# Scores and attend on 64-row array tiles for four heads at a time, with the attention written as seven rounds per group

## Chip, cores and metric

The kernel runs on one core of a Trainium2 chip. The metric is device time in microseconds of one execution of the program. Engine names below: PE is TensorE (PEld its weight loads), DVE is VectorE, ACT is ScalarE, POOL is GpSimd, SP is SyncE, which here only issues DMAs.

## What is computed

Two stages, one after the other. First attention over 8 batches of 12 heads, 448 tokens, 64 elements per head: q and k are normalised by their root mean square and scaled by `g_q` and `g_k`, then softmax of the scores times v. Its output, 3584 tokens of 768, goes through a layer of experts: a dense two-layer network for all tokens, plus one of 8 experts per token, chosen by the largest of 8 logits and weighted by its softmax probability.

```python
q_n, k_n = rmsnorm(q, g_q), rmsnorm(k, g_k)
attn = softmax(scale * q_n @ k_n.T)            # per batch and head
x = (attn @ v) as (3584, 768)
y = relu(x @ w1_dense) @ w2_dense              # 768 -> 512 -> 768
e = argmax(x @ w_gate, axis=1)
y[n] += gate[n] * (relu(x[n] @ w1[e[n]]) @ w2[e[n]])
```

## The kernel before, in words

**Tiling of the attention.** The unit is a pair of heads, `t`, 48 in all, 6 in a batch; loads go by groups of two pairs (four heads). The 448 tokens of a head lie on 112 partitions, four tokens (`JJ = 4`) in a partition. `load` (L132) brings q, k as float32 on SP's queue and v as bfloat16 on POOL's queue, three buffers each. `squares` (L155) squares on POOL (L161), sums over a head's 64 elements on DVE (L162), and every second pair makes the inverse norms on ACT (L167, L168). `normalise` (L171) multiplies on DVE (L177). `transposes` (L183) turns q and k by four 112-row transposes each on PE (L186) and copies them out of PSUM on DVE (L191 with the gains, L193).

`scores` (L196) makes one quarter `j` of the keys against all 448 queries for both heads: two matmuls, one on partitions 0 to 63 and one on 64 to 127, each 64 rows by 112 columns (L202), then one exponential over 112 x 896 on ACT (L204). `attend` (L206) multiplies the exponentials (stationary, 112 rows by 128 columns) with v and a column of ones (65 columns moving), four per 128 queries (L215); DVE divides by the ones' column (L219, L221). `xtrans` (L224) transposes the output back (L228) and ACT copies it (L230). After the last pair of a batch, `route` (L234) makes the logits (L239), the choice of expert and the gate, and writes rows of `records` in DRAM. `dense` (L301) spreads the dense network of the batch before, first layer (L273) and second (L284), over the iterations; its output goes to `records` in float32.

**Order.** PE, POOL and SP run in the written order (the `manual_schedule` at L308); DVE and ACT are ordered by the planner. In iteration `t` four steps hold `scores(t + 1, i)`, then a transpose of `t + 2` or `attend(t)`, a piece of `dense`, and `squares(t + 4)` or `normalise(t + 3)`. Expert weights are loaded through POOL's queue all along (L329). PSUM holds two scores tiles of two banks each (`a_sc`) and four single banks, tag `wk`, shared by everything else in this stage.

**Experts.** L357 to L442 count tokens by expert over all batches and give each token a place in one of 35 tiles of 128 (a one-hot selection over 4096 elements at L410, 32 matmuls at L422). Then for each tile POOL gathers 128 rows of `records` (L449: x, dense output and gate, 4864 bytes a row), PE transposes x (L460), multiplies by the expert's first matrix (L469), transposes (L479), multiplies by the second (L487, eight matmuls of 384 columns), DVE adds the dense output (L493) and POOL scatters the rows (L495).

Of the kernel before, what the change touches and what calls it, by code (L numbers as in the profile page):

```python
# [8 lines left out]
F32 = mybir.dt.float32  # L9
# [8 lines left out]
def kernel(  # L18
# [15 lines left out]
    P = 128  # L34
# [5 lines left out]
    JJ = 4  # L40
    SC = S // JJ
# [4 lines left out]
    FT = F // P  # L46
    De = D + 1
    scale = 1.0 / (D ** 0.5)
    QC = (0, 128, 256, S - 128)
# [9 lines left out]
    for hh in range(2):  # L59
        nc.sync.dma_start(gq2[hh * D:(hh + 1) * D, :], g_q.unsqueeze(1))  # L60
        nc.sync.dma_start(gk2[hh * D:(hh + 1) * D, :], g_k.unsqueeze(1))
# [4 lines left out]
    EB = E * KD * F  # L66
    NTL = N // P + E - 1
    XH = Dm // 2
    GO = XH + Dm
    NC4 = 4 * B  # L70
    tri = const.tile([P, P], BF16)
    ones = const.tile([P, P], BF16)
    nc.vector.memset(ones, 1.0)
    nc.gpsimd.affine_select(tri, ones, pattern=[[1, P]], compare_op=ALU.is_gt, fill=0.0,
                            base=0, channel_multiplier=-1)
    iop = const.tile([P, P], BF16)
    nc.gpsimd.iota(iop, pattern=[[1, P]], base=0, channel_multiplier=0,
                   allow_small_or_imprecise_dtypes=True)
    iot = const.tile([P, NTL], F32)
    nc.gpsimd.iota(iot, pattern=[[1, NTL]], base=0, channel_multiplier=0,  # L80
                   allow_small_or_imprecise_dtypes=True)
    iom = const.tile([P, NTL], F32)
    nc.vector.tensor_scalar(iom, iot, float(P), None, op0=ALU.mult)
    prio = const.tile([P, E], F32)
    nc.gpsimd.iota(prio, pattern=[[-1, E]], base=E, channel_multiplier=0,
                   allow_small_or_imprecise_dtypes=True)
    col = const.tile([P, 4], F32)
    for mi in range(4):
        nc.gpsimd.iota(col[:, mi:mi + 1], pattern=[[0, 1]], base=QC[mi], channel_multiplier=1,
                       allow_small_or_imprecise_dtypes=True)  # L90
    cmp3 = const.tile([P, 4, JJ - 1], F32)
    for jj in range(1, JJ):
        nc.vector.tensor_scalar(cmp3[:, :, jj - 1], col, float(jj * SC), None, op0=ALU.is_ge)
    colj = const.tile([P, 4], F32)
    nc.vector.tensor_reduce(colj, cmp3, AX.X, ALU.add)
    colp = const.tile([P, 4], F32)
    nc.vector.scalar_tensor_tensor(colp, in0=colj, scalar=-float(SC), in1=col,
                                   op0=ALU.mult, op1=ALU.add)
    tok = const.tile([P, B, 4, 3], BF16)
    for b in range(B):  # L100
        nc.vector.memset(tok[:, b, :, 0], float(b + 1))
        nc.vector.tensor_copy(tok[:, b, :, 1], colj)
        nc.vector.tensor_copy(tok[:, b, :, 2], colp)
    nc.vector.memset(tok[:D, :, 3, :], 0.0)

    RC = Dm // 2 + Dm + 64
    rec = nc.dram_tensor("records", (N, RC), F32).ap()
    oh = const.tile([P, B, 4, E], BF16)
    wgb = const.tile([P, KD, E], BF16)
    wd1 = const.tile([P, KD, F], BF16)  # L110
    wd2 = const.tile([P, FT, Dm], BF16)
    we = const.tile([P, E, 2, KD * F], BF16)

# [9 lines left out]
    with tc.tile_pool(name="a_ld", bufs=3) as ld, \  # L123
# [3 lines left out]
        gts = [sb.tile([P, 4, RC - GO], F32, name=f'gt{i}', tag=f'gt{i}', bufs=1) for i in range(2)]  # L127
        for gt in gts:
            nc.vector.memset(gt, 0.0)
        xin, ssqs, rs, xn, qkT, exs, vas, xnats, xTs, hTs, vrs = [{} for _ in range(11)]  # L130

        def load(g):  # L132
            if g * GP >= NT:
                return
            b, h0 = divmod(g * GP * 2, H)
            parts = ((0, 2), (2, 4)) if g == 0 else ((0, 2 * GP),)
            for name, src in (("q", q), ("k", k)):
                xin[name, g] = ld.tile([SC, 2 * GP, JJ * D], F32, tag="x" + name, name="x" + name)
            for a, z in parts:
                for name, src in (("q", q), ("k", k)):  # L140
                    nc.sync.dma_start(
                        xin[name, g][:, a:z],
                        src[b, h0 + a:h0 + z].rearrange("h (p j) d -> p h (j d)", j=JJ))
            vr = ld.tile([SC, 2 * GP, JJ * D], BF16, tag="vr")
            nc.gpsimd.dma_start(vr, v[b, h0:h0 + 2 * GP].rearrange("h (p j) d -> p h (j d)", j=JJ))
            vrs[g] = vr
            ssqs[g] = sb.tile([SC, 2, 2 * GP * JJ], F32, tag="ssq", name="ssq")

        def values(g):
            va = ld.tile([SC, 2 * GP, JJ, D + 2], BF16, tag="va")  # L150
            nc.vector.memset(va[:, :, :, D:], 1.0)
            nc.vector.tensor_copy(va[:, :, :, :D], vrs[g].rearrange("p h (j d) -> p h j d", d=D))
            vas[g] = va

        def squares(t, names="qk"):  # L155
            g, i = divmod(t, GP)
            for name in names:
                n = "qk".index(name)
                x = xin[name, g][:, 2 * i:2 * i + 2, :]
                sq = sb.tile([SC, 2, JJ * D], F32, tag="sq")  # L160
                nc.gpsimd.tensor_mul(sq, x, x)  # L161
# [62 lines left out]
        def xtrans(t):  # L224
# [6 lines left out]
            if pr == NPR - 1:  # L231
                route(b)
# [319 lines left out]
```

## Time and profile before

| what | us |
|---|---|
| median of 3 runs (515.98 to 524.04) | 519.65 |
| the profiled execution | 519.15 |
| its span, first to last instruction | 517.3 |
| busy in the span: PE / DVE / ACT / POOL | 399.3 / 326.6 / 274.8 / 205.3 |

The rows further down are of this one execution. A duration is that of one instruction as the profiler saw it; consecutive matmuls overlap, so their cost is better read from the distance of their starts. `x16` after an operation merges that many, and the time ahead is that of all of them. Text in brackets is idle time of the engine ahead of the instruction and what ended it.

### The profile page before, as it was taken

To read this page: it belongs to the slowest core of one execution; us is meant where nothing else is said; L and a number is where in the kernel's file an instruction comes from. 1 tells how busy PE (TensorE), PEld (TensorE's weight loads), DVE (VectorE), ACT (ScalarE), POOL (GpSimd) and SP (SyncE) were. 2 spreads that over 40 slices of the span, in tenths; PEclk is the share of its full clock that TensorE was granted. 3 is DMA by queue.
4 is the path that set the end of the run, shared out by engine and by line. 5 is a ranking of instruction groups with operands and counts; after the bars stand their busy time and mean duration, and the time that the engine had idled before them with its cause. 6 is when DMAs were issued, how large, how long until landed. Compare 5 with 4: busy or idle time off the path is not lost.

```text
span 517.3 us, 10774 instructions
## 1 busy us (share of the span) xinstructions
PE 399.3 (77%) x4010; PEld 232.7 (45%) x4010; DVE 326.6 (63%) x761; ACT 274.8 (53%) x431; POOL 205.3 (40%) x223
## 2 busy tenths in 40 slices
PE   0189888769688887788977979980249889899894
PEld 0046645435344454454543545650215555556552
DVE  3796999868568779588786975427603434444442
ACT  0077887648567756767855978730003333333331
POOL 6674354453426327128136130000023555556542
PEclk9999999979888989979977999996559999999998
DMA  8999679997798599959879441251063878888860
GB/s 142 237 218 175 151 154 159 192 256 96 176 269 137 137 271 142 198 133 239 187 134 248 107 144 30 81 152 46 1 241 122 278 253 266 286 283 266 294 259 2
DMA packets 66017, 92.62 MB, mean 179 GB/s; under 512 B 8749, under 2 KB 56109, under 8 KB 65968
## 3 DMA queue, kind: packets, MB, share of 16 engines
q0 software_dynamic: 31568, 52.48, 45.4%
q1 hardware_dynamic: 34400, 39.46, 27.6%
q8 instruction: 33, 0.54, 0.4%
q14 instruction: 16, 0.13, 0.1%
HBM read 83.16 MB, written 31.20 MB: 221 GB/s over the span
## 4 chain that ended last, share of the span: by engine, by line
PE 30%; DMA 27%; DVE 20%; ACT 7%; issue 6%; POOL 6%; SPq 2%; POOLq 0%; DVEq 0%; ACTq 0%
DMA xq<-in_q_dram 9%; DMA xg<-records,row 9%; DMA xk<-in_k_dram 8%; DVE y L177 7%; PE he L469 5%; PE av L215 5%; DVE ssq L162 5%; PE ps L202 5%; PE yp L487 4%; ACT ex L204 4%; POOL sq L161 4%; PE ff L273 4%; PE ff L284 2%; DVE xa L221 2%; PE tr L186 2%
## 5 line engine op out<-in xcount | busy, mean ns | idle before, releaser
L204 ACT ACTIVATE ex<-ps 112x896 bf16<-112x896 f32 x192 | 173.8, 921 | 54.3 <-PE ps L202 52.7
L161 POOL TENSOR_TENSOR sq<-xq 112x512 f32<-112x512 f32 x48 | 52.1, 1085 | 141.8 <-DMA xq<-in_q_dram 118.8
L162 DVE TENSOR_REDUCE ssq<-sq 112x8 f32<-112x512 f32 x96 | 64.0, 672 | 42.9 <-POOL sq L161 42.9
L202 PE MATMUL ps<-y 64*112 64x448 bf16 x384 | 84.1, 435 | 2.5 <-DVE y L193 1.3
L215 PE MATMUL av<-va,ex 112*128 112x65 bf16 x1536 | 71.2, 202 | 17.7 <-DVE xa L221 16.0
L215 PEld LDWEIGHTS <-ex 112*128 112x128 bf16 x1536 | 59.3, 103 | 40.9 <-DVE xa L221 21.3
L284 PE MATMUL ff<-wd,hT 128*112 128x384 bf16 x256 | 60.4, 347 | 10.8 <-DVE xa L221 10.8
L449 POOL DMA_INDIRECT xg<-records,row x35 | 33.9, 967 | 81.1 <-DVE dest L442 70.4
L186 PE MATMUL tr<-ident,y 112*128 112x112 bf16 x384 | 39.2, 232 | 29.0 <-DVE y L177 24.2
L161 POOL TENSOR_TENSOR sq<-xk 112x512 f32<-112x512 f32 x48 | 51.3, 1070 | 19.1 <-DVE ssq L162 9.8
L495 POOL DMA_INDIRECT out_dram<-ys,dest x35 | 35.6, 1018 | 58.6 <-DVE ys L493 58.6
L474 ACT ACTIVATE hs<-he,xg 128x512 bf16<-128x512 f32 x35 | 24.0, 687 | 65.6 <-DMA xg<-records,row 36.3
L469 PE MATMUL he<-we,xT 128*128 x210 | 53.5, 393 | 3.0 <-issue 1.5
L462 DVE COPY xT<-xp 128x768 bf16<-128x768 bf16 x35 | 19.5, 557 | 57.5 <-PE xp L460 57.5
L202 PEld LDWEIGHTS <-y 64*112 64x112 bf16 x384 | 26.2, 131 | 61.6 <-issue 56.0
L273 PE MATMUL ff<-xT,wd 128*128 128x448 bf16 x192 | 52.1, 373 | 2.1 <-DVE xa L221 2.1
L487 PE MATMUL yp<-we,heT 128*128 x280 | 51.2, 326 | 0.8 <-DVE ys L493 0.8
L493 DVE TENSOR_TENSOR ys<-yp,xg 128x768 f32<-128x768 f32 x35 | 33.5, 957 | 28.0 <-PE yp L487 28.0
L481 ACT COPY heT<-hp 128x512 bf16<-128x512 bf16 x35 | 20.5, 586 | 49.1 <-PE hp L479 49.1
L186 PEld LDWEIGHTS <-y 112*128 112x128 bf16 x384 | 22.9, 104 | 51.0 <-DVE y L177 25.3
L177 DVE TENSOR_TENSOR y<-xq,r 112x512 bf16<-112x512 f32 x48 | 45.0, 937 | 0.9 <-ACT r L168 0.9
L221 DVE TENSOR_TENSOR xa<-av,inv 128x256 bf16<-128x256 f32 x96 | 40.1, 418 | 1.4
(98 smaller groups left out, 473.3 us busy)
## 6 DMA issues: line engine op xcount, KB each, us to landing
we<-in_moe_w_dram POOLq DMA_DIRECT2D x16, 768.0 KB, 8.4
records<-ys SPq DMA_DIRECT2D x32, 336.0 KB, 3.3
xq<-in_q_dram SPq DMA_DIRECT2D x23, 448.0 KB, 6.7
xk<-in_k_dram SPq DMA_DIRECT2D x23, 448.0 KB, 7.0
vr<-in_v_dram POOLq DMA_DIRECT2D x24, 224.0 KB, 5.9
records<-xa SPq DMA_DIRECT2D x8, 576.0 KB, 7.4
wd<-in_moe_w_dense_dram POOLq DMA_DIRECT2D x2, 768.0 KB, 19.4
records<-xa SPq DMA_DIRECT2D x8, 96.0 KB, 7.0
```

The lines of the kernel that those rows point to most:

```text
L161: nc.gpsimd.tensor_mul(sq, x, x)
L162: nc.vector.tensor_reduce(ssqs[g][:, n, 2 * i * JJ:(2 * i + 2) * JJ], sq.rearrange("p h (j d) -> p (h j) d", d=D), AX.X, ALU.add)
L177: nc.vector.tensor_mul(y.rearrange("p j h d -> p h j d"), x.rearrange("p h (j d) -> p h j d", d=D), rs[g][:, n, 2 * i * JJ:(2 * i + 2) * J ...
L186: nc.tensor.transpose(ps[:, j * SC:(j + 1) * SC], xn[name, t][:, j].rearrange("p h d -> p (h d)"), ident[:SC, :SC])
L202: nc.tensor.matmul(ps[:, hh, :S], qkT["k", t][d0:d0 + D, j * SC:(j + 1) * SC], qkT["q", t][d0:d0 + D, :], start=True, stop=True)
L204: nc.scalar.activation(exs[t][:, j], ps[:, :, :S], AF.Exp, scale=scale)
L215: nc.tensor.matmul(av[:, mi], exs[t][:, j, hh, QC[mi]:QC[mi] + P], vas[t // GP][:, 2 * (t % GP) + hh, j, :De], start=(j == 0), stop=(j == ...
L221: nc.vector.tensor_mul(xnats[b][:, :, h * D:(h + 1) * D], av[:, :, :D], inv.to_broadcast([P, 4, D]))
L273: nc.tensor.matmul(ffs[0], wd1[:, kk, ff * P:(ff + 1) * P], xTs[b][:, kk], start=(kk == 0), stop=(kk == KD - 1))
L284: nc.tensor.matmul(ffs[0], hTs[b][:, ff, j * SC:(j + 1) * SC], wd2[:, ff, dd * Dm // 2:(dd + 1) * Dm // 2], start=(ff == 0), stop=(ff == F ...
L469: nc.tensor.matmul(he, xTs[t][:, kk], we[:, bass.ds(eregs[t], 1), 0, kk * F:(kk + 1) * F] .rearrange("p o f -> p (o f)"), start=(kk == 0), ...
L487: nc.tensor.matmul(yp[:, dd, :HD], heTs[t][:, ff], we[:, bass.ds(eregs[t], 1), 1, ff * Dm + dd * HD:ff * Dm + (dd + 1) * HD] .rearrange("p ...
```

## The change

The four heads of a group are now worked on together. The tokens of a head lie on 64 partitions, seven in each (`J = 7`); two heads are stacked on the 128 partitions (index `r`), two lie side by side (`hh`). A transpose turns 128 x 128 at once, seven for q and seven for k of the group. Scores take seven rounds: a round makes 64 keys against 448 queries for all four heads, with four matmuls of 64 rows by 64 columns; `hh` sets the rows and the PSUM bank, `r` the columns. The exponential is over 128 x 896. The exponentials' ring of 14 tiles lies in the space of the last experts' weights, so the last eight weight loads are written after the attention. Attend takes 64-row operands, two heads in turn, into two PSUM banks. There are 24 periods for 24 groups and two more, and all five engines run in the written order.

Moved: the v copy and k's product go from DVE to POOL, the copy of the output's transposes from ACT to DVE, `g_q`/`g_k` loads from SP's queue to ACT's, loads to five groups ahead. Of the dense network only the first layer stays in the attention: its output (512 bfloat16) goes into `records`, whose rows shrink from 4864 to 2816 bytes, and the second layer is eight more matmuls in each expert tile, with four more transposes. Ranks and places of tokens are made batch by batch (`ranks`, `places`) instead of all at the end.

```diff
-    JJ = 4
+    J = 7
-    RC = Dm // 2 + Dm + 64
+    GO = XH + F // 2
+    RC = GO + 64
...
+        NX = 2 * J
+        xflat = we.rearrange("p e a f -> p (e a f)")[:, -NX * 2 * S:]
...
         def values(g):
-            nc.vector.tensor_copy(va[:, :, :, :D], vrs[g].rearrange("p h (j d) -> p h j d", d=D))
+            nc.gpsimd.tensor_copy(vabs[g % 3][:, :, :, :D],
+                                  xin["v", g].rearrange("p h (j d) -> p h j d", d=D))
...
+        def normalise(g, name):
+            eng = nc.vector if name == "q" else nc.gpsimd
+            y = sb.tile([P, J, 2, D], BF16, tag="xn" + name, bufs=1)
+            for hh in range(2):
+                eng.tensor_mul(y[:, :, hh], xin[name, g][:, hh].rearrange("p (j d) -> p j d", d=D),
+                               rs[g][:, "qk".index(name), hh].unsqueeze(2)
+                               .to_broadcast([P, J, D]))
...
+            ps = scp.tile([P, 2, 512], F32, tag="sc", name="sc")
             for hh in range(2):
+                rows = slice(hh * D, (hh + 1) * D)
+                for r in range(GP):
+                    nc.tensor.matmul(ps[r * D:(r + 1) * D, hh, :S], kT[rows, r, j],
+                                     qT[rows, r].rearrange("p j s -> p (j s)"),
+                                     start=True, stop=True)
+            nc.scalar.activation(x, ps[:, :, :S], AF.Exp, scale=scale)
...
+            if m == 0:
+                for r in range(GP):
+                    avs[hh, r] = wkp.tile([P, 4, De], F32, tag="wk", name="av")
+            for j in range(J):
+                for r in range(GP):
+                    rows = slice(r * D, (r + 1) * D)
+                    nc.tensor.matmul(avs[hh, r][:, m], exs[g, j][rows, hh, QC[m]:QC[m] + P],
+                                     va[rows, hh, j, :De], start=(j == 0), stop=(j == J - 1))
...
+        def period(g):
+            b, gb = divmod(g, NB)
+            more = g + 2 < NG, g + 3 < NG
+            for i in range(J):
+                if g + 1 < NG:
+                    scores(g + 1, i)
+                relu()
+                if i == 0:
+                    if g > 1:
+                        xturned(g - 2)
+                    if more[0]:
+                        normalise(g + 2, "k")
+                        normalise(g + 2, "q")
+                    if gb != 1:
+                        fill(g, 5)
+                if i in (1, 2, 4, 5) and g < NG:
+                    for m in range(2):
+                        attend(g, i // 3, (i - 1) % 3 * 2 + m)
+                if i == 1:
+                    if more[1]:
+                        squares(g + 3, "q")
+                    if g % 2 == 0:
+                        load_v(g // 2 + 2)
+                if i == 2:
+                    while nw[0] < len(wjobs) - LATE and (nw[0] - 2) * WPACE <= g + 1:
+                        nc.gpsimd.dma_start(*wjobs[nw[0]])
+                        nw[0] += 1
+                if i == 3:
+                    if more[0]:
+                        transposes(g + 2, "q")
+                        transposes(g + 2, "k")
+                    if g < NG:
+                        divide(g, 0)
+                    if more[1]:
+                        sums(g + 3, "q", 0)
+                    if gb == 1 and g > 1:
+                        logits(b - 1)
+                    if more[1]:
+                        squares(g + 3, "k")
+                    load(g + 5)
+                if i == 4:
+                    if more[0]:
+                        turned(g + 2, "q")
+                        turned(g + 2, "k")
+                    if more[1]:
+                        sums(g + 3, "q", 1)
+                    if gb == 1 and g > 1:
+                        choose(b - 1)
+                    if more[0]:
+                        values(g + 2)
+                if i == 5 and more[1]:
+                    for hh in range(2):
+                        sums(g + 3, "k", hh)
+                if i == 6:
+                    if g < NG:
+                        divide(g, 1)
+                    if more[1]:
+                        norms(g + 3)
+                    if g > 0 and g - 1 < NG:
+                        xtrans(g - 1)
+                    if gb == 1 and g > 1:
+                        ranks(b - 1)
+                        places(b - 1)
+                    fill(g, 5)
...
+            hd = sb.tile([P, F], BF16, tag="hd", bufs=1)
+            nc.scalar.activation(hd, f, AF.Relu)
...
+                for g in range(3):
+                    for name in "qk":
+                        squares(g, name)
+                        for hh in range(2):
+                            sums(g, name, hh)
+                    norms(g)
+                    if g < 2:
+                        for name in "qk":
+                            normalise(g, name)
+                            transposes(g, name)
+                            turned(g, name)
+                        values(g)
+                    if g == 0:
+                        for j in range(J):
+                            scores(0, j)
+                    load(g + 3)
...
+                    nc.tensor.matmul(yp[:, dd, :HD], hdTs[t][:, i],
+                                     wd2[:, i, dd * HD:(dd + 1) * HD],
+                                     start=(i == 0), stop=False)
...
-            nc.vector.tensor_add(ys, yp[:, :, :HD],
-                                 xgs[t][:, XH:GO].rearrange("p (a d) -> p a d", a=2))
+            nc.vector.tensor_copy(ys[:, 0], yp[:, 0, :HD])
+            nc.scalar.copy(ys[:, 1], yp[:, 1, :HD])
```

The helpers not shown: `sums`, `norms`, `turned`, `divide`, `xtrans`, `xturned`, `logits` and `choose` are the parts of the old functions in pieces of their own; `ranks` is eight small matmuls and `places` ten DVE operations per batch; `dense(n)` is one 512-column matmul of the first layer (24 a batch), `fill(g, n)` issues up to n of them, and `relu` empties what is finished and writes it to `records` on SP's queue.

## Rows read from the trace of the kernel before

**Rows 1.** Engines by stretch: length, busy time (instructions) of each, clock, DMA share, GB/s.
```profile
core 0: us, PE busy (x) PEld busy (x) DVE busy (x) ACT busy (x) POOL busy (x), PEclk, DMA share, GB/s
...
27.40:336.00 308.60, 264.60 (x3036) 152.38 (x3037) 237.35 (x582) 223.04 (x346) 118.21 (x123) 0.93 0.79 168
...
373.90:383.10 9.20, 1.63 (x13) 1.22 (x14) 1.11 (x2) 0.00 (x0) 4.84 (x5) 0.50 0.74 242
383.10:510.40 127.30, 116.49 (x828) 67.55 (x827) 50.94 (x67) 44.54 (x70) 63.65 (x64) 0.97 0.72 241
510.40:517.30 6.90, 0.06 (x1) 0.00 (x0) 0.96 (x1) 0.00 (x0) 0.98 (x1) 0.70 0.01 0
```

**Rows 2.** The page's chain of work that ended last, by engine.
```profile
PE 30%; DMA 27%; DVE 20%; ACT 7%; issue 6%; POOL 6%; SPq 2%; POOLq 0%; DVEq 0%; ACTq 0%
```

**Rows 3.** Waits, longest first: us in total, times, longest.
```profile
POOL sq L161 <- DMA xq<-in_q_dram: 118.8, 13, 12.1
```

**Rows 4.** Order of time on PE in the attention: start, us, instruction.
```profile
191.03 0.54 PE L273 MATMUL ff<-xT,wd 128*128 128x448 bf16 x2
191.50 0.40 PE L202 MATMUL ps<-y 64*112 64x448 bf16 x2
191.83 0.68 PE L215 MATMUL av<-va,ex 112*128 112x65 bf16 x16
192.35 0.54 PE L273 MATMUL ff<-xT,wd 128*128 128x448 bf16 x2
```

**Rows 5.** Order of time on PE, early in the attention.
```profile
34.87 1.06 PE L215 MATMUL av<-va,ex 112*128 112x65 bf16 x16
```

**Rows 6.** Groups by line and shape: count, busy us, mean ns, idle before.
```profile
L204 ACT ACTIVATE ex<-ps 112x896 bf16<-112x896 f32 x192 | 173.8, 921 | 54.3 <-PE ps L202 52.7
...
L162 DVE TENSOR_REDUCE ssq<-sq 112x8 f32<-112x512 f32 x96 | 64.0, 672 | 42.9 <-POOL sq L161 42.9
...
L177 DVE TENSOR_TENSOR y<-xq,r 112x512 bf16<-112x512 f32 x48 | 45.0, 937 | 0.9 <-ACT r L168 0.9
L221 DVE TENSOR_TENSOR xa<-av,inv 128x256 bf16<-128x256 f32 x96 | 40.1, 418 | 1.4
...
L202 PEld LDWEIGHTS <-y 64*112 64x112 bf16 x384 | 26.2, 131 | 61.6 <-issue 56.0 <-DVE y L193 2.1 <-DVE inv L219 0.7
...
L191 DVE TENSOR_SCALAR y<-tr,gqk 128x448 bf16<-128x448 bf16 x48 | 21.2, 441 | 1.9 <-PE tr L186 1.5
...
L193 DVE COPY y<-tr 128x448 bf16<-128x448 bf16 x48 | 18.2, 380 | 2.7 <-PE tr L186 2.7
...
L219 DVE RECIPROCAL inv<-av 128x4 f32<-128x4 f32 x96 | 16.7, 174 | 18.3 <-PE av L215 18.2
```

**Rows 7.** Order of time on DVE and POOL in the start.
```profile
22.61 1.70 DVE L177 TENSOR_TENSOR y<-xk,r 112x512 bf16<-112x512 f32 x1
22.70 1.06 POOL L161 TENSOR_TENSOR sq<-xq 112x512 f32<-112x512 f32 x1
...
24.24 0.68 DVE L177 TENSOR_TENSOR y<-xq,r 112x512 bf16<-112x512 f32 x1
```

**Rows 8.** Order of time on PE over one tile of the expert stage.
```profile
398.35 1.46 PE L469 MATMUL he<-we,xT 128*128 x6
399.64 0.50 PE L460 MATMUL xp<-ident,xg 128*128 128x128 bf16 x6
399.98 1.46 PE L487 MATMUL yp<-we,heT 128*128 x8
401.28 0.39 PE L479 MATMUL hp<-ident,hs 128*128 128x128 bf16 x4
401.50 0.38 PE L469 MATMUL he<-we,xT 128*128 x1
```

**Rows 9.** DMA issues: KB each, median us from issue to landing.
```profile
we<-in_moe_w_dram POOLq DMA_DIRECT2D x16, 768.0 KB, 8.4
records<-ys SPq DMA_DIRECT2D x32, 336.0 KB, 3.3
```

More of the change, by code (lines that the diff above doesn't have):

```diff
@@ L82 @@
[L82 to L83 removed]
+    iom = const.tile([P, NM], F32)
     prio = const.tile([P, E], F32)
[L85 to L90, printed above, removed]
@@ new lines, in fill, with run @@
+        def fill(g, n):
+            while n > 0 and nd[0] < (g - 1) // NB * 4 * KD and nd[0] < 4 * KD * B:
+                dense(nd[0])
+                nd[0] += 1
+                n -= 1
+        nw, nd = [3], [0]
+        def run(order):
+            with tc.manual_schedule(engines=order):
+                load(0)
+                load_v(0)
+                load(1)
+                load(2)
+                constants()
+                setup()
+                for job in wjobs[:3]:
+                    nc.gpsimd.dma_start(*job)
+                for g in range(3):
+                    for name in "qk":
+                        squares(g, name)
+                        for hh in range(2):
+                            sums(g, name, hh)
[7 more added lines that the diff above has]
+                    if g == 0:
+                        for j in range(J):
+                            scores(0, j)
+                    load(g + 3)
+                load_v(1)
+                for g in range(NG + 2):
+                    period(g)
+                relu()
+                fill(10 ** 6, 10 ** 6)
+                relu()
+                while nw[0] < len(wjobs):
+                    nc.gpsimd.dma_start(*wjobs[nw[0]])
+                    nw[0] += 1
@@ L350 @@
+        run({PE, POOL, SP, DVE, ACT})
     with tc.tile_pool(name="m_sb", bufs=5) as sb, \
[L351 to L352 removed]
+         tc.tile_pool(name="m_p1", bufs=3, space=bass.MemoryType.PSUM) as ps1, \
          tc.tile_pool(name="m_p2", bufs=2, space=bass.MemoryType.PSUM) as ps2, \
[L354 removed]
+         tc.tile_pool(name="m_ph", bufs=1, space=bass.MemoryType.PSUM) as psh, \
@@ new lines @@
+        nc.vector.tensor_tensor(tl, iot3, hi.unsqueeze(1).to_broadcast([P, NTL, NC4]),
+                                ALU.is_equal)
+        val = one.tile([P, 2, NTL, NC4], BF16)
+        for i in range(2):
+            nc.vector.tensor_mul(val[:, i], tl, tok[:, i].unsqueeze(1)
+                                 .to_broadcast([P, NTL, NC4]))
+        slp = ps2.tile([P, 2, NTL], F32, tag="he")
+        for n in range(NC4):
+            nc.tensor.matmul(slp, sel[:, n // 4, n % 4], val[:, :, :, n],
+                             start=(n == 0), stop=(n == NC4 - 1))
@@ L502, in gemm2 @@
             stores.append(i)
-        eregs, stores = {}, []
-        for t in range(4):
-            gather(t)
-        with tc.manual_schedule(engines={mybir.EngineType.PE}):
+        with tc.manual_schedule(engines={PE, POOL}):
+            for t in range(4):
+                gather(t)
             for t in range(2):
```

523 lines of the change are left out of this document (232 added, 291 removed).

## Prediction

> **What bounds the kernel now.** I read the stages first, then the chain and the waits, then single lines, and last the order on TensorE inside one stretch of each stage. The stage rows [rows 1] split the span of 517.3 us into a start of 27.4, an attention stage of 308.6, a tail of 37.9 up to the first gather, and an expert stage of 143.4. In attention the work for four heads (two iterations, a "group" below; there are 24) takes 308.6/24 = 12.86 us. No engine fills that: PE is busy 264.6/24 = 11.0, DVE 9.9, ACT 9.3, POOL 4.9. The chain [rows 2] gives DMA 27% and DVE 20% beside PE's 30%, and the waits [rows 3] say why: POOL stands 118.8 us in 13 waits for q to land before it can square it; DVE's reduction waits for the square, with the divisions that free PSUM queued behind it. So attention is bound by a chain (load, square, reduce, normalise) run by engines that stall in line, not by any engine's work. In the expert stage PE is the bound: 35 tiles at 3.15 us each in a stretch without data waits [rows 8] are 110 of the 143.4.
>
> **The sum's frame.** Everything is set against the profiled execution, 519.15 us, which is its span and 1.85 around it. The median of the runs shown is 519.65, 0.1% above, so no correction is made. Their spread (515.98 to 524.04) means that 2% is about the least that can be told from no change.
>
> **TensorE per group.** Seven rounds replace eight scores steps. Today a step of two 448-column matmuls on two row halves is followed 0.33 later by the next work (191.50 to 191.83), and the pair of 448-column matmuls ahead takes 0.47 from its start to that of the scores (191.03 to 191.50) [rows 4]. One such matmul streams 448/2.4 = 0.187 at the full clock of 2.4 GHz, so the pair ahead needs 0.374 of the 0.47, and 0.10 is the change of array shape. The two scores matmuls fit into 0.33 only side by side. With four 64x64 tiles all side by side a round costs the same 0.43: 7 x 0.43 = 3.0 us. Column halves in use at once are shown nowhere; in turn they cost 0.187 more a round, 1.3 a group. I take side by side, as the row halves do. The attend step becomes 112 matmuls with 64 rows (today 64 with 112 rows). Sixteen of today's take 0.52 (191.83 to 192.35), 0.0325 each, weight load included: 112 x 0.0325 = 3.6. From below, if the two row halves overlap fully, 1.8; from above, if each load stands alone as the 64-row loads of the scores do (26.2 us over 384, 0.068 each [rows 6]), 7.6. I take 3.6, the row of the same operation. The 14 + 8 transposes at 0.34/6 = 0.057 [rows 8] are 1.25. Dense1 is now 24 matmuls of 512 columns a batch, 8 a group at 1.29/6 = 0.215: 1.7; dense2 leaves this stage. Logits and ranks, 11 small matmuls a group at the attend row's 0.0325, are 0.4. Sum: 10.0 us.
>
> **DVE per group**, from [rows 6], lengths scaled by 448/512 where the shape shrinks: four sums at 0.59 (2.35); q's two products at 0.82 (1.65); the two transposed copies of 896 as two of 448 each (1.65); four divisions, 0.418 + 0.174 (2.4); the output transposes' copy, moved here from ACT (0.75); routing a third of 19 small operations at 0.174 and one of 512 elements at 0.94 (1.4). That is 10.2, and an upper figure: consecutive rows start about 0.07 before the earlier duration has run out (22.61 + 1.70 is 24.31, the next starts at 24.24 [rows 7]), near 1.2 a group. The range on q's product is wide. It is 0.68 with POOL quiet and 1.70 beside POOL's square [rows 7], and the new order starts q's product on DVE and k's on POOL from the same wait, so both may be slow: 1.2 to 3.0 for two. I take the mean's 1.65; 3.0 takes the overlap back.
>
> **ACT and POOL.** ACT has 7 x 0.921 = 6.4 [rows 6]; with its other work of today, (223.0 - 173.8)/24 = 2.05, at most 8.5. POOL squares 4 x 0.93 = 3.7 (1.06 [rows 7] by the shape) and adds k's product (1.9 at that length, more when contended) and the value copy (no row; 0.5 to 1.9, by half and by twice the square's 0.93); with DMA issues near 9. Neither reaches PE. POOL's line now holds k's product ahead of the next squares, so a late norm holds up squares, then sums. That loop, with two sums and 0.6 for the norms, is 1.9 + 3.7 + 1.2 + 0.6 = 7.4, under the period. Loads are written five groups ahead on SP and reach a free buffer nearly two groups before use, some 18 us against at most the 8.4 in which the larger weight loads land [rows 9], so the 118.8 us wait goes. SP also carries the dense records' writes; a load queued behind one waits for a relu, a fraction of a us against that slack.
>
> **What is late next.** Four PSUM banks serve attend outputs, transposes, logits, ranks and dense. In the rounds after the first pair of heads DVE does two divisions, one sum and q's copy, 1.18 + 0.59 + 0.88 = 2.65, before a bank comes free for the second pair. PE does two rounds of scores and the transposes meanwhile, 1.66. When an unfinished dense tile holds the fourth bank, in two groups of three, PE waits 1.0. So a group is 10.0 + 0.65 = 10.65 us, from 9.8 to 12.
>
> **The whole.** Start: q and k of group 0 landed near 10 (issued by 2, at most 8.4 to land [rows 9]), then squares 3.7, sum and norms 1.2, k's product 1.9, transpose and copy 1.7, seven exponentials 6.4: 25. In the written order ACT now has to take the norms of groups 1 and 2 before it goes on, behind k's product, the value copy and the squares of group 2: 8 more, 33. Attention: 24 x 10.65, less 0.8 for group 22 and 3.8 for group 23, which lack transposes and scores: 251. Early groups run at half clock today (16 attend matmuls 1.06 at 34.87 against 0.68 at 191.83 [rows 4, 5], 1.2 against 2.4 GHz); two groups at that pace lose some 2 each: +4. That is 288. To the first gather: transposes, logits, choice, ranks and places of the last batch now run here, but scans over all batches, the 4096-wide selection and dense2 do not; some 17. Beside it four dense writes go through one buffer, each 0.6 and 3.3 to land [rows 9], about 20 in all; and eight weight loads wait for the space of the exponentials, the last three, up to 8.4 each [rows 9], ahead of the gathers on POOL's queue. I take 20 (17 to 32): 308. Expert stage: each tile gains eight 384-column matmuls (1.30, 399.98 to 401.28 as now) and four transposes (0.23): 3.15 + 1.53 = 4.68, times 35 is 164. Of the other 33.2 of today's stage, start and end (9.2 and 6.9, from the first and last tiles) stay; of the 17 of data waits and half clock I keep 5, as gathered rows shrink from 4864 to 2816 bytes while a tile takes longer: 185. End 493, and 1.85: 495 us. In short, attention gains 54 (its 309 becomes 255), the tail 18, the expert stage loses 42 and the start 6.
>
> The Trainium skill, page "TensorE: Matmul & The Clock Gate", section "Measured speedup vs the span model", has packed tiles start some 4 ns apart and end together. By it the attend step would fall to the 1.8 above; the scores pair in 0.33 agrees, no row shows it for 65 columns. That is rival one.
>
> The Trainium skill, page "TensorEngine Tiling (Array Packing)", section "Restrictions and Gotchas", says that column tiling excludes fast weight load. By the loads' 0.068 against 0.0325 that would put up to 14 x 0.068 = 0.95 a group on the scores, 23 us, if nothing covered the two further loads of a round; no run here shows it yet.
>
> **Rivals.** One: attend halves overlap. PE falls to 8.2, DVE (9.0 to 10.2) becomes the bound, near 9.8 with waits, and 24 x 0.85 = 20 goes: 475. For it, the scores pair; against, no row shows two 128-column loads at once, and the attend step has one for each matmul. Two: the engines in written order hand over as badly as now. Today's period is 12.86/11.0 = 1.17 times its busiest engine; 1.17 x 10.2 = 11.9, +30: 525. Against it, the load wait that made the ratio is gone; for it, DVE and PE are now within 2% of each other. Three: column halves run in turn, +1.3 a group, 526. Four, slower: the attend step's 64-row loads are not hidden and cost 0.068 each on PE: 7.6 for 3.6, +4.0 a group, +95, 590. It decides from 0.041 a matmul on, where 24 x 1.0 us eats the whole gain. For it, half-height loads in [rows 6] are dearer than the 0.0325 of a whole attend matmul; against, those loads follow a change of shape, which inside the attend step there is none.
>
> **Chances.** Forecast 495 (480 to 509): 0.47. One 0.13, two 0.13, three 0.10, four 0.17. Faster by over 2% (under 509.3) is the first two, 0.60; two and three lie within 2% except a spill of 0.05: 0.18; slower 0.22. The range goes from 470, past rival one, to 542, past two and three with a few us of late weights; it leaves out four and a little below.
>
> **What would show it.** Right: a group near 10.65 between repeats of a round-0 line; four scores matmuls to the next work in about 0.33; 14 attend matmuls in 0.45; POOL's wait for q gone; a PE wait on q's transposed copy; a tile near 4.7 with PE as its bound. Wrong: 28 attend matmuls taking over 1.2 us; q's product at 1.5 with DVE never idle; POOL setting the sums; the first gather waiting over 30 us on weights or records.

## The result and the profile after

The changed kernel took 501.78 us (median of 4 runs, 500.06 to 503.14) against 517.82 for the kernel before beside it: a ratio of 0.9704, 95% interval 0.9632 to 0.9776. It is 3% faster, where 495 (4.7% faster) was predicted. Some executions of a kernel take over 1.5% longer than its fastest: a ratio leaves them out, a median counts all. The profiled execution took 500.06 us, with a span of 498.4.

Engines by stretch in the changed kernel, with the columns of [rows 1]: start to the first scores, attention to the last attend, tail to the first gather, gather to the first tile, tiles, end.

```profile
0.00:18.90 18.90, 1.72 (x15) 1.33 (x16) 8.62 (x83) 1.83 (x3) 15.17 (x28) 1.00 1.02 223
18.90:282.40 263.50, 210.22 (x4238) 125.83 (x4239) 228.27 (x514) 170.27 (x246) 176.97 (x186) 0.91 0.71 167
282.40:316.80 34.40, 17.48 (x118) 9.94 (x117) 11.32 (x45) 4.30 (x8) 1.62 (x3) 0.68 0.75 151
316.80:324.40 7.60, 2.27 (x20) 2.01 (x21) 1.32 (x5) 0.00 (x0) 4.89 (x5) 0.50 0.68 195
324.40:493.10 168.70, 166.47 (x1243) 102.70 (x1240) 49.00 (x102) 57.51 (x104) 63.77 (x64) 0.98 0.40 133
493.10:498.40 5.30, 0.03 (x1) 0.00 (x0) 0.56 (x1) 0.48 (x1) 0.98 (x1) 0.81 0.01 2
```

DVE is now the busiest in attention (third of the engines in the row, 228.27 of 263.50), where [rows 1] had PE. The trace's clock record begins at 39.0, so the column's 1.00 ahead of that is no reading: 28 attend matmuls took 0.95 at 31.08 and 0.61 at 39.06. The scores of group 0 alone start at 18.9; the first period with attend begins at 30.2. Counted from there, the span's 18.9 us (517.3 to 498.4) are: start 27.4 to 30.2, 2.8 lost; attention 308.6 to 252.2, 56.4 won; tail 37.9 to 34.4, 3.5 won; expert stage 143.4 to 181.6, 38.2 lost.

The page's chain of the changed kernel, by engine and by line, against [rows 2]:

```profile
issue 30%; DVE 30%; POOL 14%; PE 13%; DMA 9%; ACT 2%; POOLq 1%; ACTq 0%; SPq 0%; DVEq 0%
DMA records<-hd 7%; POOL xg L555 7%; DVE ssq L190 6%; DVE xa L262 5%; PE av L253 5%; DVE y L204 4%; POOL sq L185 3%; PE sc L235 3%; POOL out_dram L609 3%; PE ff L351 3%; DVE y L221 2%; DVE xT L277 2%; DVE lo L338 2%; ACT hd L360 2%; DMA gk<-in_g_k_dram 1%
```

The 30% under issue, time in which the engine waited for nothing that the profile shows, lie mostly in the expert stage (71% of the chain from 316.8 on, 5% of it in the attention). DMA fell from 27% to 9%, and its first entry is no longer a load but the write of the dense records. The waits say the same: POOL's wait for q of [rows 3] is gone, and these stand in its place.

```profile
POOL y L204 <- ACT r L197: 41.4, 24, 4.2
...
ACT hd L360 <- DMA records<-hd: 32.9, 14, 7.1
...
POOL sq L185 <- DVE ssq L190: 31.6, 7, 5.5
```

Order of time on PE in a period without routing, to be held against [rows 4]:

```profile
194.86 0.38 PE L235 MATMUL sc<-y 64*64 64x448 bf16 x4
195.18 0.61 PE L253 MATMUL av<-va,we 64*128 64x65 bf16 x28
195.72 0.38 PE L235 MATMUL sc<-y 64*64 64x448 bf16 x4
```

Four scores matmuls are followed by the next work after 0.32 us. At the pace of 512 columns in 0.215 [rows 8] one of 448 columns takes 0.188, and two at a time would need 0.376: the four 64x64 tiles run side by side. The 28 attend matmuls take 0.54 (195.18 to 195.72), 0.019 each against 0.0325 before; one after the other, at that pace, their 65 columns would need 0.76, so the halves overlap. Per group that is 2.2 us instead of the predicted 3.6.

**Periods.** The distance of the scores' starts in round 0 gives the period of a group. From 30.2 to 267.5 it is 10.8 us on the mean (10.65 predicted), but the three groups of a batch differ. Over the 16 periods from 80.0 to 258.5, the first of a batch takes 8.86, the second (logits, choice, ranks and places of the batch before) 12.08, the third 12.31; together 33.2. Along the chain of waits from 80.0 to 245.9, its pieces added up by engine, 103 us are DVE's and 46 PE's. By period the chain holds 3.3 of each in the first, 11.6 of DVE in the second, and 5.8 of each in the third. What makes DVE late can be read where `places` runs. DVE first:

```profile
245.03 0.61 DVE L335 CAST ri<-rf 128x4 int32<-128x4 f32 x1
245.68 0.85 DVE L336 TENSOR_SCALAR ri<-ri 128x4 int32<-128x4 int32 x1
246.57 0.86 DVE L337 CAST tj<-ri 128x4 f32<-128x4 int32 x1
247.46 1.70 DVE L338 SCALAR_TENSOR_TENSOR lo<-tj,rf 128x4 bf16<-128x4 f32 x1
249.19 0.69 DVE L340 TENSOR_TENSOR sel<-iop,lo 128x512 bf16<-128x512 bf16 x1
249.80 0.62 DVE L277 COPY xT<-xt 128x896 bf16<-128x896 bf16 x1
```

and POOL in the same stretch:

```profile
243.79 1.83 POOL L204 TENSOR_TENSOR y<-xk,r 128x448 bf16<-128x448 f32 x2 [2.65 <-ACT r L197]
245.58 1.82 POOL L185 TENSOR_TENSOR sq<-xq 128x448 f32<-128x448 f32 x2
247.34 0.82 POOL L395 DMA_DIRECT2D we<-in_moe_w_dram  x1
248.18 0.94 POOL L185 TENSOR_TENSOR sq<-xk 128x448 f32<-128x448 f32 x1
```

An operation on four elements ends when a POOL instruction does (245.6, 246.5, 247.4, 249.1; `x2` merges two of equal length). In the tail, with POOL quiet, the same four take 0.15 to 0.17. The output copy L277 and q's product stand behind them in DVE's written order, and PE behind these. The Trainium skill has this rule, page "SBUF — State Buffer", section "Who interferes with whom": VectorE and GpSimd share one pair of ports, held for a whole instruction, and a cast or an operation with two SBUF inputs can block. The trace agrees, with 0.85 in place of 0.17. `choose` loses time likewise: its L296 took 0.75 to 1.59 in six batches and 0.19 in the two that found POOL quiet. No edit below moves it.

**Tail.** ACT after the last exponential:

```profile
286.53 0.60 ACT L360 ACTIVATE hd<-ff 128x512 bf16<-128x512 f32 x1 [7.11 <-DMA records<-hd]
292.72 0.60 ACT L360 ACTIVATE hd<-ff 128x512 bf16<-128x512 f32 x1 [5.60 <-DMA records<-hd]
299.19 0.60 ACT L360 ACTIVATE hd<-ff 128x512 bf16<-128x512 f32 x1 [5.86 <-DMA records<-hd]
299.68 0.22 ACT L304 ACTIVATE eg<-cent 128x32 f32<-128x32 f32 x1
302.09 0.60 ACT L360 ACTIVATE hd<-ff 128x512 bf16<-128x512 f32 x1 [2.19 <-DMA records<-hd]
```

A relu can't overwrite the one record buffer until its write has landed. The writes land in 5.5 to 7.0 us while the eight late weight loads run (to about 301), and in 2 after. The last batch's exponential and the PSUM banks of the dense matmuls wait behind it.

**A tile.** PE in the expert stage, against [rows 8]:

```profile
400.80 1.46 PE L577 MATMUL he<-we,xT 128*128 x6
...
402.43 0.39 PE L569 MATMUL hp<-ident,xg 128*128 128x128 bf16 x4
402.65 1.46 PE L596 MATMUL yp<-wd,hdT 128*128 128x384 bf16 x8
403.95 1.46 PE L601 MATMUL yp<-we,heT 128*128 x8
...
405.48 0.81 PE L577 MATMUL he<-we,xT 128*128 x3
```

From 400.80 to 405.48: 4.68 us a tile, the predicted figure.

### The profile page after: what moved, and what is told of

Same layout as the page of the kernel before. It is cut to its first block, busy times and chain, and to the rows that moved or that the text cites. A ratio compares the mean times of both kernels' runs of the same rounds, so it can differ in the third digit from the quotient of the medians.

```text
span 498.4 us, 13956 instructions
## 1 busy us (share of the span) xinstructions
PE 398.2 (80%) x5628; PEld 241.8 (49%) x5628; DVE 299.1 (60%) x747; ACT 234.4 (47%) x362; POOL 263.4 (53%) x285
## 4 chain that ended last, share of the span: by engine, by line
issue 30%; DVE 30%; POOL 14%; PE 13%; DMA 9%; ACT 2%; POOLq 1%; ACTq 0%; SPq 0%; DVEq 0%
DMA records<-hd 7%; POOL xg L555 7%; DVE ssq L190 6%; DVE xa L262 5%; PE av L253 5%; DVE y L204 4%; POOL sq L185 3%; PE sc L235 3%; POOL out_dram L609 3%; PE ff L351 3%; DVE y L221 2%; DVE xT L277 2%; DVE lo L338 2%; ACT hd L360 2%; DMA gk<-in_g_k_dram 1%
## 5 line engine op out<-in xcount | busy, mean ns | idle before, releaser
L238 ACT ACTIVATE we<-sc 128x896 bf16<-128x896 f32 x168 | 147.1, 919 | 63.9 <-PE sc L235 63.3
L253 PE MATMUL av<-va,we 64*128 64x65 bf16 x2688 | 68.0, 197 | 16.5 <-DVE xT L277 10.0
L235 PE MATMUL sc<-y 64*64 64x448 bf16 x672 | 69.5, 411 | 12.8 <-ACT we L238 11.4
L204 POOL TENSOR_TENSOR y<-xk,r 128x448 bf16<-128x448 f32 x48 | 52.3, 1110 | 41.4 <-ACT r L197 41.4
L253 PEld LDWEIGHTS <-we 64*128 64x128 bf16 x2688 | 53.1, 98 | 42.0 <-issue 38.7
L351 PE MATMUL ff<-wd,xT 128*128 128x512 bf16 x192 | 59.1, 449 | 12.6 <-DVE xa L262 9.3
L190 DVE TENSOR_REDUCE ssq<-sq 128x7 f32<-128x448 f32 x96 | 56.0, 609 | 4.5 <-POOL sq L185 4.3
L577 PE MATMUL he<-we,xT 128*128 (+1 forms) x210 | 53.6, 393 | 0.2 <-issue 0.2
L596 PE MATMUL yp<-wd,hdT 128*128 128x384 bf16 x280 | 51.2, 326 | 1.1 <-ACT ys L608 1.1
L601 PE MATMUL yp<-we,heT 128*128 (+1 forms) x280 | 51.2, 326 | 0.0
```

What stands on the lines that cost most here:

```text
L190: nc.vector.tensor_reduce(ssqs[g][:, "qk".index(name), hh], sqs[name, g, hh].rearrange("p (j d) -> p j d", d=D), AX.X, ALU.add)
L204: eng.tensor_mul(y[:, :, hh], xin[name, g][:, hh].rearrange("p (j d) -> p j d", d=D), rs[g][:, "qk".index(name), hh].unsqueeze(2) .to_broa ...
L235: nc.tensor.matmul(ps[r * D:(r + 1) * D, hh, :S], kT[rows, r, j], qT[rows, r].rearrange("p j s -> p (j s)"), start=True, stop=True)
L238: nc.scalar.activation(x, ps[:, :, :S], AF.Exp, scale=scale)
L253: nc.tensor.matmul(avs[hh, r][:, m], exs[g, j][rows, hh, QC[m]:QC[m] + P], va[rows, hh, j, :De], start=(j == 0), stop=(j == J - 1))
L351: nc.tensor.matmul(ff[0], xTs[b][:, kk, QC[m]:QC[m] + P], wd1[:, kk], start=(kk == 0), stop=(kk == KD - 1))
```

## Experiments

All but the first edit the changed kernel. Ratios are to the kernel before, beside which each ran; the changed kernel's is 0.9704 (0.9632 to 0.9776). Where the intervals overlap, the time alone doesn't tell the two apart, and what counts is what the trace shows.

**The load wait of before.** In the kernel before, q and k are loaded for three groups only:

```diff
-            parts = ((0, 2), (2, 4)) if g == 0 else ((0, 2 * GP),)
+            parts = ((0, 2), (2, 4)) if g == 0 else ((0, 2 * GP),) if g < 3 else ()
+                if g > 2:
+                    xin[name, g] = xin[name, g - 3]
+                    continue
```

> The kernel before, in which q and k are loaded for the first three groups of heads alone and these tiles are used again: it leaves out the other loads of q and k. The prediction's account (GpSimd's 118.8 us of waiting for q sets the 12.86 us per group): the attention stage falls from 308.6 to 260 or 275 us, near its TensorE time of 264.6. Rival (the loads wait for a buffer that VectorE's products free, so the landing is late only because the engines are; the hand-overs set the period): at most 15 us less.

491.16 us, one run, against 518.99. Its attention:

```profile
28.20:305.00 276.80, 251.47 (x3006) 146.02 (x3007) 241.74 (x578) 219.34 (x344) 120.42 (x123) 0.98 0.61 116
```

276.8 against 308.6: 31.8 us less, just short of the expected stretch and twice what the rival allows. The load wait cost about that much. A group still takes 11.5, so the rest was not loads.

**The written order of DVE and ACT.** `run({PE, POOL, SP})` in place of `run({PE, POOL, SP, DVE, ACT})`.

> The changed kernel with VectorE and ScalarE given back to the planner; TensorE, GpSimd and SyncE keep the written order. Theory A (the written order of these two is part of what brought the period from 12.86 to 10.8 us): the period goes up by 0.5 to 1.5 us, 12 to 36 us more in all, ratio 0.99 to 1.04. Theory B (the stacked tiles and the early loads bring the gain, and the order of the two engines is worth nothing or costs, since VectorE's written line is where TensorE waits): at most 5 us away, ratio 0.96 to 0.98, or lower still.

532.31 us, 1.0247 (1.0197 to 1.0297): slower than before. The three periods of a batch are 9.29, 16.76 and 11.93; POOL now waits for PE's transposes:

```profile
POOL y L204 <- PE tr L213: 84.5, 16, 8.9
```

So with DVE and ACT in the planner's order the new tiles and loads don't pay: some 30 us hang on it. What in that order costs so much was not followed beyond this wait.

**Four record buffers at the end.** The last two batches' records go in turn through q's and k's transposed tiles:

```diff
-                hd = sb.tile([P, F], BF16, tag="hd", bufs=1)
+                late = b > B - 3
+                hd = sb.tile([P, F], BF16, tag=("Tq", "Tk")[m % 2] if late else "hd", name="hd",
+                             bufs=2 if late else 1)
```

> The relu copies of the last two batches go to four buffers in turn instead of one, all else as changed. Theory A (the one buffer sets the tail: each write of a dense record takes 5.6 to 7 us to land beside the weight loads, and ScalarE, TensorE's banks and the route's exponential stand behind it): the relu's waits for the write (7.1, 5.6, 5.9 us in the profile of the changed kernel) vanish, the route of the last batch ends earlier, and the first gather is issued near 306 to 308 instead of 316.8; 9 us less, a ratio near 0.955 to before. Theory B (the eight late weight loads, which fill the DMA engines until about 301 and stand ahead of the gathers on GpSimd's queue, set the tail): the first gather stays at 313 to 317, within 3 us, ratio 0.965 to 0.970.

490.76 us, 0.9473 (0.9407 to 0.9539). The first gather went out at 307.6, as theory A had it. The last attend ended 2 us later (the borrowed tiles held up the last scores, 272.1 for 267.5), so the tail is 23.3. It still ends on one write beside the weights, in the chain:

```profile
295.82 0.60 ACT hd L362
296.43 0.02 issue
296.44 10.05 DMA records<-hd
306.49 0.02 issue
```

**Weights after the gathers.** The last four loads are issued one with each of the first four tiles; one record buffer as in the changed kernel.

```diff
-                while nw[0] < len(wjobs):
+                while nw[0] < len(wjobs) - 4:
...
+                if t < 4:
+                    nc.gpsimd.dma_start(*wjobs[len(wjobs) - 4 + t])
                 if t + 4 < NTL:
                     gather(t + 4)
```

> The last four weight loads (experts 6 and 7, first read by tile 6) are issued one by one behind the first gathers instead of at the end of attention; the dense records still go through one buffer. Theory A (the weight loads make each dense write land in 5.6 to 7 us instead of 1.8, and the one buffer only passes this on): the relus after 285 no longer wait more than 2.5 us, the first gather is issued at 303 to 306 instead of 316.8, the first gathers land sooner too: 12 to 15 us less, ratio 0.94 to 0.95. Theory B (the one buffer is the cause by itself, whatever the load): the gather at 312 to 316, ratio 0.96 to 0.97. If the tiles from 6 on wait for their weights, the expert stage grows by what they wait.

496.38 us, 0.9574 (0.948 to 0.9668). ACT in the tail:

```profile
287.78 0.60 ACT L360 ACTIVATE hd<-ff 128x512 bf16<-128x512 f32 x1 [6.38 <-DMA records<-hd]
290.23 0.60 ACT L360 ACTIVATE hd<-ff 128x512 bf16<-128x512 f32 x1 [1.85 <-DMA records<-hd]
292.65 0.60 ACT L360 ACTIVATE hd<-ff 128x512 bf16<-128x512 f32 x1 [1.82 <-DMA records<-hd]
```

Nearly as theory A says: with fewer loads in flight the waits are 1.8 to 2.9, apart from one of 6.38. The gather went out at 311.0, 27 after the last attend: between the theories. Three tiles then took 5.3, 8.1 and 5.5 instead of 4.67, 4.9 us together, since gathers now queue behind the weights. Buffer and load make the tail's excess together: neither edit alone brings it to 20 (23.3 and 27).

**The route's small operations later.** The second half of `places` (the five from L335 to L340) goes behind q's product, into round 1 of the period after:

```diff
+        def spots(b):
+            rf = trs["f"]
             ri = sb.tile([P, 4], I32, tag="ri")
...
                 if i == 1:
+                    if gb == 2 and g > 2:
+                        spots(b - 1)
```

> The second half of the route's small VectorE operations (the two casts, the shift, the place in the tile and the selection matrix) moves from round 0 of one period into round 1 of the next, behind the output transposes' copy and q's product. Theory A (these operations, 0.38 to 1.1 us each beside GpSimd's work, stand ahead of that copy and of q's product in VectorE's written order and stretch the periods with logits and ranks to 11 to 14 us, against 8.85 without): some 3 us less per batch, 8 batches, 15 to 25 us less, ratio 0.93 to 0.94. Theory B (PSUM banks, dense matmuls and the hand-overs set these periods, and VectorE merely works the same sum in another order): within 4 us of the changed kernel, ratio 0.962 to 0.972.

495.36 us, 0.9555 (0.9494 to 0.9616). Theory A's direction and about a third of its size: the third period fell from 12.31 to 10.90, the others stood, and the last attend came 5.7 us sooner.

**The same on GpSimd.** The four small ones in float32 on POOL, in round 1 behind q's squares; the selection on DVE in round 5.

```diff
+            nc.gpsimd.tensor_scalar(ri, rf, 1.0 / P, -63.5 / P, op0=ALU.mult, op1=ALU.add)
+            nc.gpsimd.tensor_scalar(tj[:, b], ri, 12582912.0, 12582912.0, op0=ALU.add,
+                                    op1=ALU.subtract)
+            nc.gpsimd.tensor_scalar(ri, tj[:, b], -float(P), None, op0=ALU.mult)
+            nc.gpsimd.tensor_add(lo[:, b], ri, rf)
```

> Four small operations of the route (tile number and place within it) go from VectorE to GpSimd, into round 1 of the period after, and the selection matrix into round 5. Theory A (VectorE's line sets the periods with routing, and work taken off it for good counts more than work moved back within it): attention shorter than with the operations merely moved, 8 to 20 us less than the changed kernel, ratio 0.93 to 0.955. Theory B (GpSimd's line, with squares behind these operations, passes the delay on through the sums): no better than the move alone, ratio 0.955 to 0.97.

497.87 us, 0.9607 (0.9512 to 0.9702); the three periods are 8.86, 12.22 and 11.12. DVE does 15 us less than with the move alone (135.6 against 150.4 over 15 periods) and nothing is gained by it, as theory B said. So DVE's busy time is not what the third period waits for once the operations stand further back; whether POOL's longer line (120.5 for 116.5) passes the delay on was not separated.

**The same in a quiet round.** In round 6 of that period, behind the norms.

```diff
                         norms(g + 3)
+                    if gb == 2 and g > 2:
+                        spots(b - 1)
```

> The five small operations of the route that were moved into round 1 stand in round 6 of that period instead, behind the norms, where GpSimd is idle for some 2 us. Theory A (each such operation, with all operands in SBUF, ends only when the GpSimd instruction beside it does: 0.61, 0.85, 0.86, 1.70 us in the changed kernel, 0.89, 0.86, 0.17, 0.16 when moved to round 1): they take 0.16 to 0.2 each here, the third kind of period falls from 12.31 us (10.90 when moved to round 1) to 9.3 to 10.2, and the time to a ratio of 0.935 to 0.95. Theory B (only their place ahead of the output copy and q's product matters): the third kind of period stays at 10.7 to 11.1, ratio 0.952 to 0.962.

500.11 us, 0.9659 (0.9626 to 0.9692). DVE, then POOL:

```profile
223.43 0.16 DVE L339 CAST ri<-rf 128x4 int32<-128x4 f32 x1
223.63 0.17 DVE L340 TENSOR_SCALAR ri<-ri 128x4 int32<-128x4 int32 x1
223.83 0.79 DVE L341 CAST tj<-ri 128x4 f32<-128x4 int32 x1
224.65 0.85 DVE L342 SCALAR_TENSOR_TENSOR lo<-tj,rf 128x4 bf16<-128x4 f32 x1
```

```profile
223.64 1.85 POOL L204 TENSOR_TENSOR y<-xk,r 128x448 bf16<-128x448 f32 x2 [2.04 <-ACT r L197]
```

The first two run while POOL is idle and take 0.16; the next two meet k's product, released by the norms just ahead, and take 0.8. That shows the mechanism within one sequence. The third period fell to 9.78, as theory A said, but the first rose from 8.86 to 11.42, where the output copy and q's product now stand behind them: 33.1 for the three, as without the edit. The delay moved.

**The output copy back on ACT.** `nc.scalar.copy` for `nc.vector.tensor_copy` in `xturned`.

> The copy of the output transposes, which the change moved to VectorE, goes back to ScalarE (24 of 0.615 us), at the same place of the order. Theory A (VectorE's line, 89% busy in the attention stage, sets the periods): 8 to 15 us less in attention, ratio 0.94 to 0.955. Theory B (TensorE, the banks and the hand-overs set them; VectorE's copy is hidden): no change within 4 us, or up to 10 us more, since 24 copies of about 0.9 us now stand ahead of exponentials: ratio 0.965 to 0.99.

501.59 us, 0.9668 (0.9556 to 0.978): no difference that the times can tell. The periods are 9.69, 11.86 and 12.03. ACT's 0.91 a copy lengthens the first by 0.83, and the 0.6 taken off DVE shortens the others by 0.2 to 0.3.

**More work for TensorE.** The output transposes twice:

```diff
-                for m in range(4):
+                for m in (0, 1, 2, 3, 0, 1, 2, 3):
```

> Each of the output transposes is made twice into the same place: 8 more transposes a period, 8 x 0.057 = 0.46 us, 24 times, 11 us of TensorE work more. Theory A (TensorE sets the periods, as the prediction had it): 9 to 13 us more, ratio 0.988 to 0.996. Theory B (VectorE sets them and TensorE waits for it): under 4 us more, ratio 0.968 to 0.978. Between the two, each sets some of the periods.

506.53 us, 0.9785 (0.968 to 0.989): between the theories in time. The last attend ended 8.4 us later, of the 11 added; three periods took 34.5 for 33.2. By kind, four of the five first periods took 9.30 for 8.86, all but 0.02 of the 0.46 added; the fifth, 12.67, holds a record's write of 6.6. The two routed periods shifted, to 10.96 and 13.56, and together took 24.5 for 24.4, though 0.92 was added. So PE sets the period without routing, as the prediction had it, but not the sum of the routed two.

**k's product back on VectorE.** `eng = nc.vector` for both.

> k's product goes back from GpSimd to VectorE, ahead of q's. Theory A (VectorE's busy time is the limit in the periods with routing): two products of 0.7 to 1.0 us more on VectorE a period, less what q's product and the small operations gain from a quiet GpSimd: 0.8 to 1.6 us a period, 20 to 38 us in all, ratio 1.01 to 1.045. Theory B (what VectorE loses beside GpSimd is as much as the product costs): within 8 us of the changed kernel, ratio 0.96 to 0.985.

512.25 us, 0.9881 (0.9853 to 0.991), 10 more: between the theories, nearer to B. DVE's busy time over the span did not rise with 48 products more (297.7 for 299.1): q's product takes 0.71 on the mean and k's 0.75, where q's took 1.00 beside POOL's. This is what PE's transposes wait for:

```profile
L213 PE MATMUL tr<-ident,y 128*128 128x128 bf16 x336 | 29.8, 250 | 57.4 <-DVE y L204 31.4 <-ACT hd L360 26.0
```

Of the 31.4 us for the products, 23.1 lie ahead of the first attend; after it they are 8.3, against 2.3 in the changed kernel. The 26.0 were 4.1 there: the transposes stand behind relus that wait for the one record buffer, and five of its writes landed in 4.2 to 7.6 us. The three periods take 35.0: the first 13.79 for 8.86, with these waits, the second 11.51 for 12.08, the third 9.70 for 12.31. So this run doesn't price k's product. The record waits alone grew by 22 us, twice the 10 that were lost; by that estimate the product may even belong on DVE, but with more record buffers it was not tried.

**Together.** Record buffers, later small operations (round 1), and the last four weight loads behind five gathers:

```diff
-            for t in range(4):
+            for t in range(5):
                 gather(t)
+            for job in wjobs[-4:]:
+                nc.gpsimd.dma_start(*job)
```

> Three edits together: four buffers for the last dense records, the last four weight loads behind the first five gathers, and the small operations of the route in round 1 of the next period. Theory A (they remove different waits, or the same wait from both sides): last attend near 278, first gather at 295 to 300, the expert stage as long as now: 476 to 482 us, ratio 0.918 to 0.93. Theory B (each removes part of one and the same tail, and the weights that come later make tiles wait): 485 to 490 us, ratio 0.935 to 0.945.

484.46 us, 0.9273 (0.9204 to 0.9341): theory A by the ratio, with the median of all four 2 us above its range. Then with two record buffers throughout, and four only in the last batch:

> The three edits together once more, with two buffers for every dense record instead of one, and the four that borrow other tiles only in the last batch (they delayed the last scores by 4 us before). Theory A (the single buffer also stops ScalarE inside attention whenever a record's write falls beside a weight load: one such write took 7.15 us in the profile of the three edits, and the periods after it 13 to 14 us instead of 11): the third kind of period goes back to 10.9, the last attend to 274 to 278, the time to 472 to 479 us, ratio 0.91 to 0.925. Theory B (those periods are long for VectorE's sake, whatever the record's buffer): within 4 us of the three edits, ratio 0.922 to 0.935.

480.42 us, 0.9273 (0.922 to 0.9326), the ratio that theory B gave. In its profile the third period is 11.08 and the last attend ends at 273.9, about as theory A had it. The gather goes out at 293.6, a tail of 19.7. One tile takes 9.1 for its gather behind the weights. Timed, the two versions can't be told apart. Both beat both kernels.

## Why the prediction was right, and where it was not

Three steps of the forecast held: side-by-side scores, no load wait, tiles of 4.68. A period near 10.65 came out as a mean only. The time is inside 480 to 509.

- **Start.** 33 predicted, 30.2 measured.
- **Attention.** 33 to 288 predicted (255), 30.2 to 282.4 measured (252). The sum was right, its parts were not, and that they cancelled was luck. *TensorE's 10.0* was too high: the attend term, 3.6, is 2.2, nearer to the 1.8 of rival one. The span model of the Trainium skill ("TensorE: Matmul & The Clock Gate", section "Measured speedup vs the span model") gave that 1.8 in the prediction. A period without routing holds 8.2 us of PE work at full clock. *VectorE's 10.2* came true on the mean (152.8 us over the 15 periods from 80.0), but spread unevenly: 7.8 in the first period of a batch, 11.6 and 11.1 in the two routed ones. There the small operations (16 and one of 512 elements in the kernel, nine of them in `places`, where 19 and ten were counted) were priced at 0.174, the row of an operation that reads PSUM, while four of them took 0.50 to 1.10 on the mean. The prediction saw this contention for q's product, bounded it there, and did not carry it to the routing. *The bank wait*, 0.65 a group or 16 us in all, failed as a term: PE waited for q's transposed copy 2.6 us in all, and 10.0 for the output copy. So the 10.65, PE plus this wait, hid two kinds of period: 8.86 that PE sets, and over 12 on a chain that runs through DVE. That is why rival one's premise came true without its 475.
- **Rival two** (hand-overs, 11.9 a period) is the nearest to what binds in the routed periods: taking work off DVE (the copy, the small operations) gave no more than moving it, and work added on PE cost 0.1 of 0.92 there. By how much each hand-over counts stays open.
- **Tail.** This step failed: 20 predicted, 34.4 measured, above even its range of 17 to 32. The text had four dense writes of 0.6 + 3.3 each beside the weight loads. Two things were missed: writes took 5.5 to 7.0 beside those loads, and seven relus, not four, came after the last attend, with the route's exponential behind three of them in ACT's written order. With more buffers and half of the late loads out of the way the tail was 19.7.
- **Expert stage.** 185 predicted, 181.6 measured. The tile was exact, the 5 kept for waits were 4.9; the gather to the first tile took 7.6 where 9.2 was kept.
- **Rivals three and four** fell with the scores' 0.32 and the attend's 0.019. The rule of the Trainium skill that column tiling excludes fast weight load ("TensorEngine Tiling (Array Packing)", section "Restrictions and Gotchas") cost nothing visible: with four loads a round, the next work still starts 0.32 after the scores.

Where the gain went: attention gained 56, the dense second layer's 1.53 x 35 = 54 of PE time moved to the expert stage and cost 38 net, and the tail gave 3.5 of the 18 that were expected of it.

## What to carry to other kernels

When a kernel is put into a written order, ask of each instruction what stands behind it on its engine while it waits: here a four-element cast and a one-buffer write each held up the engines behind them. Price an operation by a row with the same neighbours as it will have, not by the same operation in a quiet stretch. Before moving work off the busiest engine, move it back in that engine's line first; here that gave no less (0.9555) than taking it off (0.9607).

## What the runs showed of the hardware

- The attend loads' overlap: two 64-row halves, each matmul with its own 128-column load, pass at 0.019 us a matmul, where 112-row ones took 0.0325.
- PE's clock follows the stalls. Two periods, the third of one batch and the first of the next:

```profile
178.50:192.40 13.90, 10.34 (x173) 6.17 (x172) 12.23 (x24) 7.24 (x10) 6.13 (x8) 0.75 0.56 127
192.40:201.30 8.90, 8.21 (x174) 4.92 (x174) 8.02 (x18) 7.47 (x11) 7.81 (x8) 1.00 0.43 87
```

the granted clock (third number from the end) was 0.75 and 1.00, the lower one a mix of the levels 1.2 and 2.4 GHz. PE in the first of them:

```profile
184.17 0.93 PE L253 MATMUL av<-va,we 64*128 64x65 bf16 x27 [3.56 <-DVE xT L277]
185.03 0.59 PE L235 MATMUL sc<-y 64*64 64x448 bf16 x4
185.55 0.95 PE L253 MATMUL av<-va,we 64*128 64x65 bf16 x28
```

After 3.56 us of waiting for the output copy the scores took 0.52 to the next start instead of 0.32, until 189. For as many matmuls, 173 and 174, PE was busy 10.34 and 8.21: a late DVE is paid for twice.
- L338 above, with two SBUF inputs, lasted 1.70, across a DMA issue of POOL (0.82) and the square after it. It did so in the four batches in which POOL issued a DMA there, and took 0.85 in the two in which it didn't. With the operations moved to round 1 the shift, with one SBUF input, stood at that place: 1.70 to 1.71 in four batches with an issue, 0.86 in two without. That an issue alone holds it up was not tried.
